# Sparse attention feeding a gated MLP: where batch 2's last products, the last x and the output stores are placed

## The chip, the core and the metric

The kernel runs on one core of one Trainium2 chip, in one launch. The core has TensorE (matrix products into PSUM), VectorE, ScalarE and GpSimd (elementwise work; GpSimd can't reach PSUM) and SyncE, which here only issues DMAs. The traces call them PE (with its weight loads as PEld), DVE, ACT, POOL and SP; SPq and ACTq are the DMA instructions that SyncE and ScalarE issue. The metric is the time of one execution on the device in microseconds (us), the median of several runs. Beside it stands one execution recorded by the hardware profiler, and its trace.

## The reference

For four batches, eight heads, 768 positions and a head size of 64, block-sparse attention is computed, and its result goes into a gated MLP with a spatial product (gMLP).

```python
scores = scale * np.matmul(q, k.transpose(0, 1, 3, 2))
mask = np.abs(blk_i - blk_j) <= window        # and first/last blocks, and 3 sampled blocks a row
scores = np.where(mask, scores, -1e9)
attn = softmax(scores)                        # exp, over the sum
x = (attn @ v).transpose(0, 2, 1, 3).reshape(B, S, H * D)

h = np.maximum(x @ w_in, 0.0)                 # 512 -> 1024
u, v = h[..., :512], h[..., 512:]
v_n = (v - v.mean(-1)) / np.sqrt(v.var(-1) + 1e-06)
v_s = np.einsum('ts,bsd->btd', w_spatial, v_n) + b_spatial[None, :, None]
out = (u * v_s) @ w_out
```

Inputs and output are float32; the kernel multiplies in bf16.

## The kernel before

**Attention.** The program is written as one list of slots (the loop at L880), and each engine works its instructions off in the order in which this loop issues them. Heads are taken in pairs; there are 16 pairs, four a batch, so pair 15 (heads 30 and 31 of 32) is the last of all. Slots 0 to 35 are a special start with thirds of the first batch. From slot 36 (`S0`) to 179 each slot does one chunk of 128 keys of one head: `qk_full` (L481) makes two matmuls of 384 columns into a scores' tile (PSUM tag "sc", two tiles) and ScalarE's exponential (L491). Seven slots later (`LAG`) `av_full` (L533) makes one AV group, six matmuls of 65 columns for one chunk of queries. After the sixth, `normalize` (L500) on VectorE divides by the sums (L502, L503) into xn. The last AV group of all, of head 31, is in slot 186.

**x.** gMLP wants x with features on the partitions, so a pair's xn is transposed into xt. For pairs up to 14, `xtr_dma` (L568) does this with a DMA transpose on SP's queue. For pair 15 `last_x` (L825) does it with six transposes on TensorE (L302) and two copies on VectorE.

**gMLP.** A batch is a list of steps, one matmul with 512 columns each (`product`, L608, the matmul at L615). For chunk t of six: v_t and u_t are four steps each (one for each pair of the batch, in the order of the pairs), s_t is six (the spatial product over all v), o_t is four. Together 108 steps. What follows a product:

- v_t: relu (in the last batch by ScalarE, L645), then on VectorE statistics and their aggregation (L650, L651). After each third v GpSimd computes 1/std of three chunks (L654, L656); from then on VectorE scales them, one at a time (L673, through the helper at L188), at step counts that are set when the third v closes (`vn_due`, `VN_AGE` 9, `VN_STEP` 2). What has not come up by s0 is scaled right before it.
- u_t: relu by ScalarE (L681).
- s_t: VectorE adds the bias and multiplies by u (L687). After s1, s3 and s5 a DMA transpose on SP's queue (L697) turns two chunks into `gt`, the input of the o products; in the last batch chunks 4 and 5 go one by one.
- o_t: a copy by ScalarE or VectorE into an output tile (`osb`), for batch 2 by ScalarE for t = 0, 2, 4; then a store (L716).

**Where the steps go.** `deal` (L742) queues a batch's steps and spreads them evenly over a number of slots; `run_queue` takes the next ones after the AV group of each slot. Batches 1 and 2 begin at slots 98 and 146, with 48 slots each. Within a slot the order is: scores, AV group, what `when` has put at this slot, then steps. In slot 188 `last_x` runs the rest of the queue at once (the leftovers of batch 2) and opens the last batch with the first three steps of v0, v1 and u0, before the fourth ones, which need pair 15's x. The rest of the last batch follows after the loop.

**PSUM.** `moe_ps` (L598) gives the tile for a product: within the slots in turn one of two gMLP tiles (names "ps_moe"). From `last_x` on (`ended`) it goes round three kinds: a scores' tile ("ps_sc"), an AV tile or a gMLP tile (both "ps_t").

**Weights.** w_spatial comes in six pieces, loaded by `ws_load` (L576) in slots 16 to 18: four single ones and the last two in one DMA. GpSimd casts them (L585) in slots 19 to 29.

Of the kernel before, what the change touches and what calls it, by code (L numbers as in the profile page):

```python
# [10 lines left out]
FP32 = mybir.dt.float32  # L11
# [15 lines left out]
def kernel(  # L27
# [16 lines left out]
    nc = tc.nc  # L44

    B, H, S, D = q.shape
# [3 lines left out]
    NCH = S // 128  # L50
# [6 lines left out]
    NG = H // 2  # L57
    NP = B * NG
# [6 lines left out]
    TW = TC * 128  # L65
    S0 = NT * NG * 3
# [4 lines left out]
    work = ctx.enter_context(tc.tile_pool(name="work", bufs=1))  # L71
    psum = ctx.enter_context(tc.tile_pool(name="psum", bufs=1, space=bass.MemoryType.PSUM))
# [147 lines left out]
    def dve_copy(o, i):  # L220
        nc.vector.tensor_copy(out=o, in_=i)  # L221
# [68 lines left out]
    moe_tags, held = deque(["moeA", "moeB"]), set()  # L290

    def moe_tag():
        moe_tags.rotate(1)
        if moe_tags[0] in held:
            moe_tags.rotate(1)
        return moe_tags[0]

    def bank(nm="ps", tag=None):
        return psum.tile([128, 1024], BF16, tag=tag or moe_tag(), bufs=2 if tag else 1, name=nm)

    def tr(ps, c, in_):
        nc.tensor.transpose(out=ps[:, c * 128:(c + 1) * 128], in_=in_, identity=ident)  # L302

    def pair_of(src, c):
        return src[:, c].rearrange("p h d -> p (h d)")
# [145 lines left out]
    a_ref, av_ref, x_ref, xn_ref, xt_ref = {}, {}, {}, {}, {}  # L451
# [96 lines left out]
    def xt_tile(p):  # L548
        if p not in xt_ref:
            xt_ref[p] = work.tile([128, S], BF16, tag="xt", bufs=7, name="xt")  # L550
        return xt_ref[p]
# [22 lines left out]
    ws = {}  # L574

    def ws_load(i, n=1):  # L576
        t = work.tile([128, n, S], FP32, tag=f"ws_f{n}", bufs=4 if n == 1 else 1, name="ws_f")
        nc.sync.dma_start(out=t, in_=moe_w_spatial.rearrange("(p c) s -> p c s", c=NCH)[:, i:i + n])
        for k in range(n):
            ws["f", i + k] = t[:, k]  # L580
# [17 lines left out]
    def moe_ps(last):  # L598
        if not (last or ended):
            return psum.tile([128, 512], FP32, tag=moe_tag(), bufs=1, name="ps_moe")  # L600
        tail_tags.rotate(1)
        if tail_tags[0] == "sc":
            return psum.tile([128, 1024], FP32, tag="sc", bufs=2, name="ps_sc")[:, 0:512]
        if tail_tags[0] == "moe":
            return psum.tile([128, 512], FP32, tag=moe_tag(), bufs=1, name="ps_t")
        return psum.tile([128, 512], FP32, tag="av", bufs=2, name="ps_t")

    def product(n, lhs, rhs, last, done, w=512):  # L608
        ref = {}
        out = []  # L610
        for i in range(n):
            def run(i=i):
                if i == 0:
                    ref["ps"] = moe_ps(last)
                nc.tensor.matmul(out=ref["ps"][:, 0:w], lhsT=lhs(i), rhs=rhs(i),  # L615
                                 start=(i == 0), stop=(i == n - 1))
                if i == n - 1:
                    done(ref["ps"][:, 0:w])
            out.append(run)
        return out  # L620
# [6 lines left out]
    class Moe:  # L627
# [75 lines left out]
        def o_product(self, tcc):  # L703
            steps = []
            osb = {}
            parts = 2 if self.last and tcc == NCH - 1 else 1
            w = DM // parts
            for i in range(parts):
                cs = slice(i * w, (i + 1) * w)

                def done(ps, i=i, cs=cs):
                    if i == 0:
                        osb["t"] = work.tile([128, DM], FP32, tag="osb", bufs=6, name="osb")
                    on_act = (tcc + i) % 2 == 0 if self.last else tcc in O_ACT[self.b]
                    (act_copy if on_act else dve_copy)(osb["t"][:, cs], ps)
                    (nc.scalar if i or (self.last and tcc == 0) else nc.sync).dma_start(  # L716
                        out=out[self.b].rearrange("(p c) d -> c p d", c=NCH)[tcc][:, cs],
                        in_=osb["t"][:, cs])
                steps += product(NDH, lambda d: self.gt[:, tcc, d, :],
                                 lambda d, cs=cs: w_out_t[:, d, cs], self.last, done, w)  # L720
            return steps
# [20 lines left out]
    def deal(steps, slots):  # L742
        queue.extend(steps)
        pace["slots"], pace["credit"] = slots, 0.0
# [14 lines left out]
    moe = {}  # L759
# [4 lines left out]
    def when(slot, *fns):  # L764
        at.setdefault(slot, []).extend(fns)

    def c(f, *a, **kw):
        return lambda: f(*a, **kw)
# [21 lines left out]
    def moe_begin(b):  # L790
        moe[b] = Moe(b)

    SEQ = "v0 v1 u0 v2 u1 v3 u2 v4 v5 u3 u4 u5"
# [21 lines left out]
    when(42, lambda: deal(moe[0].in_steps("v4 v5 u4 u5", TC) + moe[0].rest_steps(),  # L815
                          S0 + 8 + 48 - 42))
    for b in (1, 2):
        s0 = S0 + 48 * b + 14
        when(s0, c(moe_begin, b),
             lambda b=b: deal(moe[b].in_steps(SEQ, 3) + moe[b].rest_steps(), 48))  # L820

    last_steps = []


    def last_x():  # L825
        moe_begin(B - 1)
        m = moe[B - 1]
        ended.append(True)
        while queue:
            queue.popleft()()  # L830
        seq = m.in_steps("v0 v1 u0 v2 v3 v4 v5 u1 u2 u3 u4 u5", 3)
        n = NG - 1
        for i in (0, 1):
            for f in seq[i * NG:i * NG + n]:
                f()
        ps, xn = bank(), xn_ref.pop(("p", NP - 1))
        moe_tags.rotate(1)
        for cc in range(NCH):
            tr(ps, cc, pair_of(xn, cc))
        xt = xt_tile(NP - 1)  # L840
        for cs in (slice(0, TW), slice(TW, S)):
            dve_copy(xt[:, cs], ps[:, cs])
        for f in seq[2 * NG:2 * NG + n]:
            f()
        for i in (0, 1, 2):
            seq[i * NG + n]()
        last_steps.extend(seq[3 * NG:])

    def slot_of(p):
        return S0 + 12 * (p - NG)  # L850

    for p in range(NG, NP):
        g = slot_of(p)
        when({4: 13, 5: 22, 6: 31}.get(p, g - 34), c(load, p, "k"), c(load, p, "q"), c(load, p, "v"))
        when({4: 18, 5: 26, 6: 38}.get(p, g - 24),
             c(cast, p, "k", PL), c(cast, p, "q", PL), c(cast, p, "v", PL))
        when({4: 20, 5: 31}.get(p, g - (16 if p in (10, 14) else 20)), c(tr_dma, p))
        when(31 if p == 4 else g - (7 if p in (9, 13) else 5), c(split, p, 0))
        when(32 if p == 4 else g - 3, c(split, p, 1))
        if p == NP - 1:  # L860
            when(g + 20, last_x)
        else:
            when(g + (19 if p % NG == NG - 1 else 20), c(xtr_dma, p))
    for i, (ld, ca) in enumerate([(16, 19), (16, 21), (17, 23), (17, 25), (18, 27), (18, 29)]):
        if i < 5:
            when(ld, c(ws_load, i, 2 if i == 4 else 1))
        when(ca, c(ws_cast, i))
    for i, sl in enumerate((23, 27, 31)):
        when(sl, c(ws_tr, i))
# [60 lines left out]
```

## Time and profile before

| what | us |
|---|---|
| median of 3 runs | 209.9 (209.7 to 210.19) |
| the profiled execution | 209.46 |
| its span, first to last instruction | 207.7 |
| TensorE busy | 201.7 |
| ScalarE busy | 166.9 |
| VectorE busy | 128.9 |
| GpSimd busy | 74.5 |

Busy times are those of the span. Matmuls overlap in TensorE, so a row's length is more than its share: a matmul's time there is better read from the start of the next. A row of a timeline has the start, the length, the engine, the line, the operation, what it writes and reads, the count that was merged into it, and in brackets how long its engine had idled and what ended that. "Landing" is the time from a DMA's issue until its data has arrived.

### The profile page before, as it was taken

The page shows a single profiled execution, that of the slowest core. Times are in us where ns is not written, and L with a number is a line of the kernel's source. Part 1 is how long each engine was busy: PE and PEld are TensorE (multiplying, and loading weights), DVE is VectorE, ACT ScalarE, POOL GpSimd, SP SyncE. Part 2 cuts the span into 40 slices and gives each one's busy share as a digit, 9 for nine tenths or more (in the row PEclk, how much of TensorE's full clock was granted, in tenths as well). Part 3 has the DMA queues.
Part 4 walks back from the last instruction along what each step waited for, and adds up shares of the span by engine and source line. Part 5 has one row for each costly group of instructions (what it writes and reads, how often), then busy time and mean ns, then how long its engine had stood idle before and what let it go on. Part 6 is the DMA issues. An engine that isn't in the chain of part 4 may idle for free.

```text
span 207.7 us, 5257 instructions
## 1 busy us (share of the span) xinstructions
PE 201.7 (97%) x2128; PEld 126.8 (61%) x2128; DVE 128.9 (62%) x287; ACT 166.9 (80%) x222; POOL 74.5 (36%) x117
## 2 busy tenths in 40 slices
PE   7899999999999999999999999999999999999992
PEld 6689778756666666665556555556555655444441
DVE  7688697789644454558797445448785345476541
ACT  5999999999999999889999878988999882276021
POOL 6999898585680421400726303100201000012000
PEclk9999999999999999999999999999999999999999
DMA  5999999999999999999948548994101063810475
GB/s 138 355 364 365 359 402 248 234 270 332 275 292 246 206 302 209 324 282 280 298 54 225 143 91 261 189 267 91 31 3 38 3 88 67 286 55 0 50 186 219
DMA packets 65579, 42.21 MB, mean 203 GB/s; under 512 B 46740, under 2 KB 60436, under 8 KB 65556
## 3 DMA queue, kind: packets, MB, share of 16 engines
q1 hardware_dynamic: 64980, 41.30, 77.3%
q10 hardware_dynamic: 576, 0.59, 0.9%
q8 instruction: 16, 0.26, 0.5%
q14 instruction: 7, 0.06, 0.1%
HBM read 24.38 MB, written 6.29 MB: 148 GB/s over the span
## 4 chain that ended last, share of the span: by engine, by line
PE 92%; ACT 5%; DVE 1%; issue 0%; ACTq 0%
PE ps_moe L615 32%; PE ps L487 23%; PE ps_av L538 13%; PE ps_t L615 9%; PE ps L474 6%; ACT a_all L479 4%; PE ps_sc L615 4%; PE ps_av L520 4%; PE wps L182 1%; PE ps L302 1%; PE ps_av L302 1%; DVE osb L221 0%; ACT kq L224 0%; PE mq L309 0%; ACT osb L224 0%
## 5 line engine op out<-in xcount | busy, mean ns | idle before, releaser
L491 ACT ACTIVATE a_all<-ps 128x768 bf16<-128x768 f32 x144 | 112.7, 811 | 11.9 <-PE ps L487 5.4
L487 PE MATMUL ps<-kq 88*128 88x384 bf16 x288 | 70.4, 325 | 0.0
L538 PEld LDWEIGHTS <-a_all 128*128 128x128 bf16 x864 | 45.2, 97 | 20.0
L538 PE MATMUL ps_av<-vv,a_all 128*128 128x65 bf16 x864 | 49.8, 193 | 0.0
L487 PEld LDWEIGHTS <-kq 88*128 88x128 bf16 x288 | 27.8, 97 | 29.2 <-issue 0.3
L615 PE MATMUL ps_moe<-w_in_t,xt 128*128 128x512 bf16 x144 | 43.2, 378 | 0.0
L479 ACT ACTIVATE a_all<-ps 128x1024 bf16<-128x1024 f32 x36 | 34.1, 1028 | 1.8 <-PE ps L474 1.5
L615 PE MATMUL ps_moe<-vn,w_spt 128*128 128x512 bf16 x108 | 33.5, 378 | 0.0
L654 POOL TENSOR_SCALAR std<-mv 128x3 f32<-128x3 f32 (+1 forms) x9 | 2.9, 318 | 71.7 <-DVE mv L651 57.1
L138 POOL CAST nat<-st_k 128x768 bf16<-128x768 f32 (+2 forms) x18 | 13.8, 770 | 31.3 <-DMA st_k<-in_k_dram 31.0
L502 DVE RECIPROCAL rc<-ps_av 128x6 f32<-128x6 f32 (+1 forms) x36 | 6.7, 187 | 26.5 <-PE ps_av L538 23.7
L687 DVE SCALAR_TENSOR_TENSOR un<-ps_moe,b_col,un 128x512 bf16<-128x512 f32 x18 | 13.5, 749 | 14.8 <-PE ps_moe L615 14.8
L474 PE MATMUL ps<-kq 88*128 88x256 bf16 (+3 forms) x140 | 21.6, 275 | 1.0 <-ACT a_all L479 0.5
L615 PEld LDWEIGHTS <-xt 128*128 128x128 bf16 x192 | 15.4, 98 | 7.5 <-DVE xt L221 0.2
L503 DVE TENSOR_TENSOR xn<-ps_av,rc 128x384 bf16<-128x384 f32 (+1 forms) x36 | 18.5, 513 | 1.2
L615 PE MATMUL ps_moe<-w_out_t,gt 128*128 128x512 bf16 x60 | 17.6, 378 | 0.0
L650 DVE BATCH_NORM_STATS2 stats<-vn 128x6 f32<-128x512 bf16 x24 | 16.4, 684 | 1.3 <-ACT vn L645 0.9
L474 PEld LDWEIGHTS <-kq 88*128 88x128 bf16 (+1 forms) x140 | 12.7, 97 | 5.4 <-DVE kq L221 1.0
L138 POOL CAST nat<-st_q 128x768 bf16<-128x768 f32 (+2 forms) x21 | 14.4, 688 | 2.7 <-DMA st_q<-in_q_dram 2.2
L188 DVE TENSOR_SCALAR vn<-ps_moe 128x512 bf16<-128x512 f32 x18 | 12.3, 686 | 4.6 <-PE ps_moe L615 4.5
L615 PEld LDWEIGHTS <-w_spt 128*128 128x128 bf16 x144 | 11.7, 98 | 5.2
L221 DVE COPY kq<-tt 64x1536 bf16<-64x1536 bf16 x24 | 13.9, 581 | 0.4
(85 smaller groups left out, 207.4 us busy)
## 6 DMA issues: line engine op xcount, KB each, us to landing
st_v<-in_v_dram SPq DMA_DIRECT2D x16, 384.0 KB, 5.6
st_k<-in_k_dram SPq DMA_DIRECT2D x15, 384.0 KB, 4.7
out_dram<-osb SPq DMA_DIRECT2D x22, 256.0 KB, 2.7
st_q<-in_q_dram SPq DMA_DIRECT2D x12, 384.0 KB, 4.6
w_f<-in_moe_w_in_dram SPq DMA_DIRECT2D x6, 256.0 KB, 6.7
ws_f<-in_moe_w_spatial_dram SPq DMA_DIRECT2D x4, 384.0 KB, 7.3
w_f<-in_moe_w_out_dram SPq DMA_DIRECT2D x4, 256.0 KB, 4.0
st_q<-in_q_dram SPq DMA_DIRECT2D x6, 128.0 KB, 5.3
```

The costliest lines, as they stand in the source:

```text
L138: eng.tensor_copy(out=dst, in_=src)
L188: nc.vector.tensor_scalar(out=out, in0=in0, scalar1=s1, scalar2=s2, op0=o0, **kw)
L221: nc.vector.tensor_copy(out=o, in_=i)
L474: nc.tensor.matmul(out=ps[:, at:at + n * TW], lhsT=kq[0:kr, h, ci * 128:(ci + 1) * 128], rhs=kq[0:kr, h, qcols(t0, n)], start=True, stop=True)
L479: nc.scalar.activation(out=out, in_=ps, func=AF.Exp, scale=0.125)
L487: nc.tensor.matmul(out=ps[:, hf * 512:hf * 512 + HALF], lhsT=kq[0:KR, j % H, ci * 128:(ci + 1) * 128], rhs=kq[0:KR, j % H, S + hf * HALF:S ...
L491: nc.scalar.activation(out=a_ref["h", j][:, ci, :].rearrange("p (b c) -> p b c", b=2), in_=ps.rearrange("p (b c) -> p b c", b=2)[:, :, 0:H ...
L503: nc.vector.tensor_tensor(out=out, in0=ps[:, :, 0:D], in1=rc[:, 0:n].to_broadcast([128, n, D]), op=ALU.mult)
L538: nc.tensor.matmul(out=av_ref[j][:, qc, 0:VA], lhsT=a_ref["h", j][:, ci, qc * 128:(qc + 1) * 128], rhs=vv[p % NVV][:, h, ci, 0:VA], start= ...
L615: nc.tensor.matmul(out=ref["ps"][:, 0:w], lhsT=lhs(i), rhs=rhs(i), start=(i == 0), stop=(i == n - 1))
L650: nc.vector.bn_stats(out=stats, in_=self.vn[:, tcc, :])
L687: nc.vector.scalar_tensor_tensor(out=self.un[:, tcc, :], in0=ps, scalar=b_col[:, tcc:tcc + 1], in1=self.un[:, tcc, :], op0=ALU.add, op1=AL ...
```

## The change

Six edits.

1. `moe_ps`: batch 2's leftovers in slot 188 take scores' tiles alone (two of them, in turn); the last batch goes round the three kinds as before.
2. Pair 15's x is made by `xtr_dma`, in slot 186, right behind the AV group there; TensorE's six transposes and the two copies go. Pairs 7 and 11 move from 19 to 18 slots after their first one.
3. The last batch begins v0 v1 v2 u0 instead of v0 v1 u0 v2; the three products opened ahead are v0, v1, v2.
4. Batch 2's gMLP begins at slot 150 instead of 146, still over 48 slots; batch 1's is spread over 52.
5. The stores of o1 and o2 of the last batch are issued by ScalarE, as that of o0 was.
6. Pieces 2 and 3 of w_spatial come in one DMA, as 4 and 5 did.

```diff
     def ws_load(i, n=1):
-        t = work.tile([128, n, S], FP32, tag=f"ws_f{n}", bufs=4 if n == 1 else 1, name="ws_f")
+        t = work.tile([128, n, S], FP32, tag=f"ws_f{n}", bufs=2, name="ws_f")
...
     def moe_ps(last):
         if not (last or ended):
             return psum.tile([128, 512], FP32, tag=moe_tag(), bufs=1, name="ps_moe")
+        if not last:
+            return psum.tile([128, 1024], FP32, tag="sc", bufs=2, name="ps_sc")[:, 0:512]
         tail_tags.rotate(1)
...
-                    (nc.scalar if i or (self.last and tcc == 0) else nc.sync).dma_start(
+                    (nc.scalar if i or (self.last and tcc < 3) else nc.sync).dma_start(
...
     for b in (1, 2):
-        s0 = S0 + 48 * b + 14
+        s0 = S0 + 48 * b + (14 if b == 1 else 18)
         when(s0, c(moe_begin, b),
-             lambda b=b: deal(moe[b].in_steps(SEQ, 3) + moe[b].rest_steps(), 48))
+             lambda b=b: deal(moe[b].in_steps(SEQ, 3) + moe[b].rest_steps(), 52 if b == 1 else 48))
...
-        seq = m.in_steps("v0 v1 u0 v2 v3 v4 v5 u1 u2 u3 u4 u5", 3)
-        n = NG - 1
-        for i in (0, 1):
+        seq = m.in_steps("v0 v1 v2 u0 v3 v4 v5 u1 u2 u3 u4 u5", 3)
+        n, opened = NG - 1, 3
+        for i in range(opened):
             for f in seq[i * NG:i * NG + n]:
                 f()
-        ps, xn = bank(), xn_ref.pop(("p", NP - 1))
-        moe_tags.rotate(1)
-        for cc in range(NCH):
-            tr(ps, cc, pair_of(xn, cc))
-        xt = xt_tile(NP - 1)
-        for cs in (slice(0, TW), slice(TW, S)):
-            dve_copy(xt[:, cs], ps[:, cs])
-        for f in seq[2 * NG:2 * NG + n]:
-            f()
-        for i in (0, 1, 2):
+        for i in range(opened):
             seq[i * NG + n]()
-        last_steps.extend(seq[3 * NG:])
+        last_steps.extend(seq[opened * NG:])
...
+        when(g + (18 if p % NG == NG - 1 else 20), c(xtr_dma, p))
         if p == NP - 1:
             when(g + 20, last_x)
-        else:
-            when(g + (19 if p % NG == NG - 1 else 20), c(xtr_dma, p))
     for i, (ld, ca) in enumerate([(16, 19), (16, 21), (17, 23), (17, 25), (18, 27), (18, 29)]):
-        if i < 5:
-            when(ld, c(ws_load, i, 2 if i == 4 else 1))
+        if i not in (3, 5):
+            when(ld, c(ws_load, i, 2 if i > 1 else 1))
```

## The prediction

> **What bounds the kernel now.** I read the page first, then the chain of waits near its end, then the timelines of single engines after the last scores, at 170 us and later.
>
> ```profile
> PE 201.7 (97%) x2128; PEld 126.8 (61%) x2128; DVE 128.9 (62%) x287; ACT 166.9 (80%) x222; POOL 74.5 (36%) x117
> PE 92%; ACT 5%; DVE 1%; issue 0%; ACTq 0%
> ```
>
> TensorE is busy for 97% of the span and is 92% of the chain that ended last. The ends of matmuls are modelled, so I check it by starts. In the chain, by start and length:
>
> ```profile
> 176.62 0.69 DVE osb L221
> ...
> 181.40 0.34 PE ps L302 x6
> ...
> 190.80 2.59 PE ps_t L615 x12
> ```
>
> A gMLP step (one matmul with 512 columns) takes 2.59/12 = 0.216 us. The six transposes of pair 15's x take 0.34 us. Once, at 176.62, the chain leaves TensorE for a copy of an output tile (o1) by VectorE, which holds a PSUM bank. What this costs stands in TensorE's own timeline:
>
> ```profile
> 173.87 0.59 PE L615 MATMUL ps_moe<-w_out_t,gt 128*128 128x512 bf16 x2
> 174.30 0.35 PE L538 MATMUL ps_av<-vv,a_all 128*128 128x65 bf16 x6
> 174.49 0.59 PE L615 MATMUL ps_moe<-w_out_t,gt 128*128 128x512 bf16 x2
> 174.92 0.34 PE L538 MATMUL ps_av<-vv,a_all 128*128 128x65 bf16 x6
> 175.10 0.60 PE L615 MATMUL ps_moe<-w_out_t,gt 128*128 128x512 bf16 x2
> 175.54 0.34 PE L538 MATMUL ps_av<-vv,a_all 128*128 128x65 bf16 x6
> 175.72 1.46 PE L615 MATMUL ps_moe<-w_out_t,gt 128*128 128x512 bf16 x6
> 177.36 0.81 PE L615 MATMUL ps_t<-w_out_t,gt 128*128 128x512 bf16 x3 [0.18 <-DVE osb L221]
> ```
>
> Six steps from 175.72 end at 175.72 + 6 x 0.216 = 177.02, and the next starts at 177.36: a hole of 0.34 us. Elsewhere in these rows starts follow each other by steps alone. So TensorE is the limit, and the change can only take away matmuls or holes, or make new holes. Moving steps from one slot to another is neutral as long as nothing else becomes the limit.
>
> **The change, part by part.**
>
> *x of pair 15 by DMA* takes six transposes from TensorE: -0.34 us. Its landing (2.7 to 2.8 us for such transposes late in the run, row below) is covered by 16 steps of leftovers, 3.45 us, and nine of the last batch; without that cover what is missing of the 2.8 us would stand before v0's fourth step.
>
> *Leftovers in the scores' tiles.* The hole of 0.34 us was a wait for the bank of o1; o2 and o3 now get scores' tiles, which no exponential uses any more: -0.34 us. But there are two such tiles for five products, so o3 waits for o1's copy. By the o1 copy below (0.68 us on VectorE) it ends about 3.46 us, and o3 wants to start at 3.43 us, after the last AV group's start; with 0.06 us from copy to matmul (177.30 to 177.36) that is +0.09. Bounds: nothing, and 0.34 again.
>
> *Batch 2 four slots later.* By the kernel's own dealing arithmetic 22 steps instead of 13 are left when slot 188 flushes the queue. The slots between get fewer steps: batch 1 has 108 steps in 52 slots, 2.08 a slot.
>
> ```profile
> 110.53 1.52 ACT L491 ACTIVATE a_all<-ps 128x768 bf16<-128x768 f32 x2
> 111.93 0.60 ACT L681 ACTIVATE un<-ps_moe 128x512 bf16<-128x512 f32 x1
> ```
>
> Two exponentials back to back take 111.93 - 110.53 = 1.40 us, so ScalarE needs 0.70 us a slot and at most 0.60 more for a copy. TensorE needs 2.08 x 0.216 + 0.18 (AV, 175.54 to 175.72) + two score matmuls of 0.16 (384/512 of a step) = 0.95 us. ScalarE stays below it: no cost, and up to 0.3 us if three u copies in a row were uncovered.
>
> The cost lies at the end. s5 of batch 2 now ends in slot 187, right behind the last AV group of slot 186, and o4 and o5 read what the DMA transpose of chunks 4 and 5 writes after s5. On SP's queue this transpose now stands *behind* the new transpose of pair 15, which waits for head 31's normalisation.
>
> ```profile
> 174.14 0.75 DVE L687 SCALAR_TENSOR_TENSOR un<-ps_moe,b_col,un 128x512 bf16<-128x512 f32 x1 [0.68 <-PE ps_moe L615]
> ...
> 176.15 0.56 DVE L503 TENSOR_TENSOR xn<-ps_av,rc 128x384 bf16<-128x384 f32 x1
> 176.62 0.68 DVE L221 COPY osb<-ps_moe 128x512 f32<-128x512 f32 x1
> ```
> ```profile
> 174.92 1.23 SPq L697 DMA_TRANSPOSE gt<-un  x1
> ```
> ```profile
> 198.19 2.54 SPq L697 DMA_TRANSPOSE gt<-un  x2
> ```
> ```profile
> gt<-un SPq DMA_TRANSPOSE x1, 3.3
> ```
> ```profile
> DMA to landing us min/median/max: 2.5/3.4/4.2
> ```
> ```profile
> DMA to landing us min/median/max: 2.7/2.8/2.8
> ```
>
> The third of these is the landing of the pair issued between 196 and 198 us; the fourth that of all 13 gt transposes, the last that of the x transposes after 100 us. Count from the end of s5, which is the last AV group's start plus 0.18 plus three steps, 0.83 us. *DMA path*: head 31's xn ends 1.17 us after that AV group's start (175.54 to 176.71), so at 0.34. SP issues 0.03 later (174.89 to 174.92), at 0.37, and is held for 1.23: 1.60. The next issue follows after 0.08 (2.54 - 2 x 1.23), at 1.68; s5's own multiplication (0.75, behind xn) is done by then, at 1.09. Landing 3.3 later: 4.98. I take 3.3 of 2.5 to 4.2 because there, too, another transpose was in flight. *TensorE's path*: 16 steps, 3.45, plus 0.09: 3.54. **Hole before o4: +1.44** (0.64 to 2.34 by the landing's ends). In the kernel before, s5 ended at 173.87, three AV groups and the hole lay in between, and SP was free at once: there a landing of 3.3 would have just met o4, at 174.92 + 3.3 against 177.36 + 4 x 0.216 = 178.22. That cover is what the change uses up. Behind the waiting weights load stands all of the last batch; on SP, behind the pair, the stores of batch 2, for which nobody waits.
>
> A rule speaks for a shorter landing. A window of half a microsecond inside the data of such a pair, with the rate in GB/s last:
>
> ```profile
> 172.00:172.50 0.50, 0.50 (x9) 0.35 (x8) 0.45 (x2) 0.00 (x0) 0.00 (x0) 1.00 1.11 214
> ```
>
> At 214 GB/s the pair's 262 KB take 1.22 us. The Trainium skill ("DMA: Bandwidth & Descriptors", Latency and other measured facts) gives DMA transposes with contiguous rows about 350 to 400 GB/s. By that page I estimate 0.7 us for the data and a hole smaller by 0.5; the trace disagrees with its 214, and decides.
>
> *v2 ahead of u0 in the last batch.* Its normalisations run on VectorE in the order of the program. Write S for a chunk's statistics, V for its scaling. Before: S0 S1 S2 S3 S4 V0 V1 S5 V2. v2 now closes at step 12 instead of 16, its scalings are due at steps 20, 22 and 24, so: S0 S1 S2 S3 V0 V1 S4 V2 S5.
>
> ```profile
> 185.58 0.18 DVE L651 BATCH_NORM_AGGREGATE mv<-stats 128x2 f32<-128x6 f32 x1
> ...
> 186.38 0.18 DVE L651 BATCH_NORM_AGGREGATE mv<-stats 128x2 f32<-128x6 f32 x1
> ...
> 187.27 0.70 DVE L188 TENSOR_SCALAR vn<-vn,mv,rstd 128x512 bf16<-128x512 bf16 x2
> ...
> 190.18 1.06 DVE L188 TENSOR_SCALAR vn<-vn,mv,rstd 128x512 bf16<-128x512 bf16 x3 [1.09 <-POOL rstd L656]
> ```
> ```profile
> 186.17 0.88 POOL L656 TENSOR_TENSOR rstd<-std,mhalf 128x3 f32<-128x3 f32 x1
> ```
> ```profile
> 190.64 1.67 PE L615 MATMUL ps_t<-vn,w_spt 128*128 128x512 bf16 x7
> ```
>
> VectorE runs this stretch without a break. Now V0 stands after S3 and needs GpSimd's result, 187.05 - 185.58 = 1.47 us after S2's aggregation starts; S3 takes only 0.80 of it (185.58 to 186.38) and about 0.1 to the next start, so VectorE waits about 0.6. One scaling more (0.70/2 = 0.35) stands ahead of S5. The last V ends 0.6 + 0.35 later against TensorE. It ended at 191.24, and the sixth step of s0, which reads it, started at 190.64 + 5 x 0.216 = 191.72: a margin of 0.48. **Hole in s0: +0.5.** Bounds: 0 (all within the margin) and 0.7.
>
> *Stores 1 and 2 by ScalarE.* Each costs its queue 0.35 us:
>
> ```profile
> 200.15 0.35 ACTq L716 DMA_DIRECT2D out_dram<-osb  x1
> 201.25 0.60 ACT L224 ACTIVATE osb<-ps_sc 128x512 f32<-128x512 f32 x1 [1.13 <-PE ps_sc L615]
> ```
>
> Store 1 waits there for VectorE's copy, and ScalarE's copy of o2 waits behind it, about 0.2 us; ScalarE idles 1.13 us ahead of that copy, and o2's bank is not needed again. Cover gone, it would cost 0.35 once. I take 0. *The merged weight piece* and pair 7's and 11's x one slot earlier:
>
> ```profile
> 36.10 0.90 POOL L138 CAST nat<-st_k 128x768 bf16<-128x768 f32 x1 [0.74 <-DMA st_k<-in_k_dram]
> ```
>
> GpSimd's cast of the third piece may wait for the fourth, now in the same transfer; GpSimd idles 0.74 us at 36 us and swallows that. SP waits up to one slot longer on the two x transposes, with about eight slots until o4 of the batch ahead reads its own. I take 0, bounds -0.2 and +0.3.
>
> **The sum:** -0.34 - 0.34 + 0.09 + 1.44 + 0.5 = +1.35 us. The profiled execution took 209.46 us (span 207.7); it becomes 210.8. The three timed runs have a median of 209.9, 0.44 above it, so I predict 209.9 + 1.4 = **211.3 us**; with landings of 3.0 to 3.8 and the ends of the small terms, 210.8 to 212.0.
>
> **Rivals.** (a) *Only the hole before o4*: VectorE's chain keeps its margin, the 0.5 goes: 210.8. For: a 0.48 margin exists. Against: the new order is fixed by step counts. (b) *A short landing*: with the lowest, 2.5 us, the hole is 0.64 and the sum +0.55: 210.5. For: the row has it. Against: single chunks, half the data, are among the 13. The rate on the page of the Trainium skill named above ("DMA: Bandwidth & Descriptors") points this way, and the window's 214 GB/s against it. (c) *The pair lands in time*, the other side: if chunks 4 and 5 land under 1.86 us after their issue (3.54 - 1.68), there is no hole at o4. Then -0.59 remains, 209.3; with VectorE's 0.5 it is 209.8. It decides from a hole of 0.59 downward. For: the kernel before shows no wait at o4. Against: no landing below 2.5. (d) *A slow issue*: one gt transpose held SP for longer,
>
> ```profile
> 165.43 2.45 SPq L697 DMA_TRANSPOSE gt<-un  x1
> ```
>
> and 1.2 us more before o4 gives 212.5.
>
> **Chances.** Forecast 0.58, (a) 0.10, (b) 0.08, (c) 0.18, split 0.12 at 209.3 and 0.06 at 209.8, (d) 0.06. About 0.2%, 0.42 us, is what a measurement of this kernel can tell from no change. So faster 0.12, same 0.06, slower 0.82. Leaving out (c)'s faster part and (d), 0.18 together, the range is 209.8 to 212.0.
>
> **What would show it.** The six transposes and the 0.34 hole gone; about 0.1 before o3 on a scores' tile; a weights load of o4 waiting on the gt DMA for about 1.4 us, with the pair's issue right behind pair 15's; V0 waiting for GpSimd after S3, and s0's fourth to sixth steps late by 0.5 in all. Wrong it would be if o4 starts on time, if V0 does not wait, or if holes appear between 100 and 170 us, where I expect none.

## The result, and the profile after

The changed kernel takes **210.68 us** (10 runs, 210.32 to 210.94) beside 209.93 of the kernel before (10 runs, 209.59 to 210.31). The ratio of the times is 1.0034, with a 95% interval of 1.0025 to 1.0044: slower by 0.75 us, where +1.4 was forecast. The time lies inside the range of 209.8 to 212.0, and just under the narrower one of 210.8 to 212.0 that went with the forecast itself.

The page of the changed kernel: the span, the busy times, and the shares of the chain that ended last.

```profile
span 208.9 us, 5244 instructions
...
PE 202.2 (97%) x2122; PEld 126.5 (61%) x2122; DVE 129.6 (62%) x285; ACT 166.7 (80%) x222; POOL 73.9 (35%) x117
...
PE 87%; DVE 4%; ACT 4%; DMA 1%; POOL 1%; issue 1%; POOLq 0%; ACTq 0%
```

TensorE has six instructions fewer, the transposes. Its share of the chain fell from 92% to 87%; a DMA and GpSimd have come in, and VectorE's share has grown. The chain itself, by start and length, shows where:

```profile
176.58 3.10 DMA gt<-un
179.73 1.90 PE ps_sc L617 x8
...
187.36 0.89 POOL rstd L658
188.28 0.73 DVE vn L188 x2
```

The first line is the transpose that o4 waits for, the second o4 and o5 behind it; the last two are GpSimd's result and V0, which waits for it. How much of them is idle TensorE stands in its timeline (start, length, and in brackets the idle time and what ended it):

```profile
174.05 0.34 PE L538 MATMUL ps_av<-vv,a_all 128*128 128x65 bf16 x6
...
174.87 1.03 PE L617 MATMUL ps_moe<-w_out_t,gt 128*128 128x512 bf16 x4
175.74 2.83 PE L617 MATMUL ps_sc<-w_out_t,gt 128*128 128x512 bf16 x12
179.73 1.90 PE L617 MATMUL ps_sc<-w_out_t,gt 128*128 128x512 bf16 x8 [1.16 <-DMA gt<-un]
```

A row of n steps without a gap has the length 0.216 n + 0.16; the 0.16 is the modelled drain of the last one. Twelve would take 2.75, and the second row has 2.83: a hole of 0.08 lies in it, the one before o3. Its last step gives way at 175.74 + 2.83 - 0.16 = 178.41, and the next starts at 179.73: a hole of 1.32 before o4. SP's queue shows why:

```profile
175.28 1.21 SPq L569 DMA_TRANSPOSE xt<-xn  x1
176.58 1.26 SPq L699 DMA_TRANSPOSE gt<-un  x1
```

The gt transpose of chunks 4 and 5 is issued 0.09 us after pair 15's has let SP go, and lands 3.10 later. And s0 and s1 of the last batch, in TensorE's timeline once more:

```profile
191.83 3.23 PE L617 MATMUL ps_t<-vn,w_spt 128*128 128x512 bf16 x12
194.89 1.46 PE L617 MATMUL ps_sc<-vn,w_spt 128*128 128x512 bf16 x6
```

Twelve steps in 3.23 instead of 2.75: 0.48 us of holes (three of 0.26, 0.11 and 0.11). VectorE's timeline has their origin:

```profile
186.78 0.18 DVE L653 BATCH_NORM_AGGREGATE mv<-stats 128x2 f32<-128x6 f32 x1
186.87 0.66 DVE L652 BATCH_NORM_STATS2 stats<-vn 128x6 f32<-128x512 bf16 x1
187.57 0.18 DVE L653 BATCH_NORM_AGGREGATE mv<-stats 128x2 f32<-128x6 f32 x1
188.28 0.73 DVE L188 TENSOR_SCALAR vn<-vn,mv,rstd 128x512 bf16<-128x512 bf16 x2 [0.53 <-POOL rstd L658]
```

V0 waits 0.53 us for GpSimd behind S3 (186.87 to 187.75) and starts 1.50 us after the aggregation of S2 has started.

On TensorE the change therefore costs -0.34 - 0.34 + 0.08 + 1.32 + 0.48 = +1.20 us. The time grew by 0.75 only. The other 0.45 is not on TensorE; the experiments had to find it.

### The profile page after: what moved, and what is told of

Same layout as the page of the kernel before. It is cut to its first block, busy times and chain, and to the rows that moved or that the text cites. A ratio compares the mean times of both kernels' runs of the same rounds, so it can differ in the third digit from the quotient of the medians.

```text
span 208.9 us, 5244 instructions
## 1 busy us (share of the span) xinstructions
PE 202.2 (97%) x2122; PEld 126.5 (61%) x2122; DVE 129.6 (62%) x285; ACT 166.7 (80%) x222; POOL 73.9 (35%) x117
## 4 chain that ended last, share of the span: by engine, by line
PE 87%; DVE 4%; ACT 4%; DMA 1%; POOL 1%; issue 1%; POOLq 0%; ACTq 0%
PE ps_moe L617 31%; PE ps L487 23%; PE ps_av L538 13%; PE ps L474 6%; PE ps_t L617 5%; PE ps_av L520 4%; PE ps_sc L617 3%; ACT a_all L479 3%; DVE stats L652 1%; DMA gt<-un 1%; PE wps L182 1%; DVE kq L221 1%; DVE vn L188 1%; PE ps_av L302 1%; DVE mv L653 0%
## 5 line engine op out<-in xcount | busy, mean ns | idle before, releaser
L656 POOL TENSOR_SCALAR std<-mv 128x3 f32<-128x3 f32 (+1 forms) x9 | 2.4, 270 | 72.5 <-DVE mv L653 70.3
L617 PE MATMUL ps_moe<-w_out_t,gt 128*128 128x512 bf16 x52 | 15.6, 378 | 0.0
L221 DVE COPY kq<-tt 64x1536 bf16<-64x1536 bf16 x24 | 14.4, 598 | 0.3
```

## The experiments

Each kernel was timed beside the kernel before; a ratio stands with its 95% interval. The sum over a profile is made with the last row of TensorE and the span; the time of the profiled executions is 1.8 to 2.0 us above their spans.

### The kernel before, once more

The kernel is unchanged.

> The kernel before, unchanged, for a second profile of it. Theory: the holes that TensorE has after 20 us are fixed by the order of the program (0.34 us before o3 of batch 2, none in s0 of the last batch), and the profile shown of before is 0.47 us under its median because of its first ten microseconds, where it has 3.34 us of holes and the changed kernel 3.79. So the holes after 170 us stay within 0.1 us of 0.40 + 0.14, the first ten microseconds may move by half a microsecond, and the last 0.36 us stall of SyncE after all landings comes again or not, which tells whether it belongs to the kernel. Rival: o4 of batch 2 is a near miss in the kernel before (landing 0.3 us ahead of need), so in other executions it too waits at o4; then a hole of 0.1 to 0.5 us stands there. Time: ratio 1.000, 209.9 us.

Measured: 209.99 us, ratio 0.9995 (0.9981 to 1.0010). This profile, at 209.99, has the median's time, where the one on which the prediction rests was 0.5 under it. The six steps and o3, as predicted from the other one at 175.72 and 177.36:

```profile
176.22 1.46 PE L615 MATMUL ps_moe<-w_out_t,gt 128*128 128x512 bf16 x6
177.86 1.89 PE L615 MATMUL ps_t<-w_out_t,gt 128*128 128x512 bf16 x8 [0.18 <-DVE osb L221]
```

The hole is the same (177.86 - 176.22 - 1.30 = 0.34), and both rows stand 0.50 later: the difference arose in the first 6 us of the trace, and has nothing to do with the part that is changed. Adding the sum to the median, not to the profiled time, was the right choice.

### The order of the last batch put back

```diff
-        seq = m.in_steps("v0 v1 v2 u0 v3 v4 v5 u1 u2 u3 u4 u5", 3)
+        seq = m.in_steps("v0 v1 u0 v2 v3 v4 v5 u1 u2 u3 u4 u5", 3)
```

> The changed kernel with the last batch's order v0 v1 u0 v2 put back (opened ahead: v0, v1, u0). Theory: the three holes in s0 (0.26 + 0.11 + 0.11 us) come from V0 waiting behind S3 for GpSimd and one scaling more ahead of S5; they go, nothing else changes: 0.48 us less than the changed kernel, 210.2 us. The hole before o4 stays at 1.2 to 1.4 us. Rival: what is late in s0 only moves on, to the gt transposes before o2 and o5 of the last batch; then the time stays at 210.7.

Measured: 210.08 us, ratio 1.0002 (0.9990 to 1.0015); 0.60 less than the changed kernel. TensorE's timeline of this kernel:

```profile
191.94 2.75 PE L617 MATMUL ps_t<-vn,w_spt 128*128 128x512 bf16 x12
194.53 1.46 PE L617 MATMUL ps_sc<-vn,w_spt 128*128 128x512 bf16 x6
```

Twelve steps in 2.75, no hole; the one before o4 stays at 1.32. So the +0.5 in s0 is caused by the order alone.

### Pair 15's transpose issued behind that of chunks 4 and 5

```diff
+        if p == NP - 1:
+            late.setdefault(g + 19, []).append(c(xtr_dma, p))
+        else:
+            when(g + (18 if p % NG == NG - 1 else 20), c(xtr_dma, p))
-        when(g + (18 if p % NG == NG - 1 else 20), c(xtr_dma, p))
```

> The changed kernel with the DMA transpose of pair 15's x issued behind that of chunks 4 and 5 of batch 2 (end of slot 187 in place of slot 186). Theory: the transpose of chunks 4 and 5 then starts when s5's multiplication ends, 1.12 us after the end of s5 instead of 1.71, lands 3.15 later, and the hole before o4 shrinks from 1.32 to about 0.7 us: 210.1 us. Pair 15's x lands about 5.2 us after s5 and is needed at 7.9. Rival: the landing and not the queue sets it, or two transposes in flight slow each other in this order too; then the hole stays over 1.1 us and the time at 210.6 or more.

Measured: 210.17 us, ratio 1.0019 (1.0002 to 1.0037). SP and TensorE:

```profile
176.57 1.23 SPq L699 DMA_TRANSPOSE gt<-un  x1
177.90 1.26 SPq L569 DMA_TRANSPOSE xt<-xn  x1
```
```profile
176.81 2.40 PE L617 MATMUL ps_sc<-w_out_t,gt 128*128 128x512 bf16 x10
179.83 1.90 PE L617 MATMUL ps_sc<-w_out_t,gt 128*128 128x512 bf16 x8 [0.62 <-DMA gt<-un]
```

The hole is now 179.83 - (176.81 + 2.40 - 0.16) = 0.78. It fell by 0.54, and the median time by 0.51. The times alone would not carry this: the interval overlaps that of the changed kernel (1.0025 to 1.0044), and the profiled execution, at 210.74, is not shorter, since its TensorE had fallen 0.5 us behind already between 31 and 39 us, far ahead of the edit. The hole is the evidence. So 0.54 of the 1.32 is the place behind pair 15's issue, and 0.78 is there without it: then s5's own multiplication, behind xn on VectorE, sets the issue (it ends at 176.54).

### Batch 2 back at its old slots, the rest of the change kept

```diff
-        s0 = S0 + 48 * b + (14 if b == 1 else 18)
+        s0 = S0 + 48 * b + 14
...
-             lambda b=b: deal(moe[b].in_steps(SEQ, 3) + moe[b].rest_steps(), 52 if b == 1 else 48))
+             lambda b=b: deal(moe[b].in_steps(SEQ, 3) + moe[b].rest_steps(), 48))
```

> The changed kernel with batch 2 at its old place (slot 146, batches 1 and 2 over 48 slots each); all other edits stay. Theory: s5 ends in slot 183 with three AV groups behind it and SyncE free, so the hole before o4 falls to 0 to 0.35 us; the hole before o3 (0.34 before) stays gone, the six transposes stay gone, the 0.48 us in s0 stay. So 1.0 to 1.3 us under the changed kernel: 209.4 to 209.7 us, at or just under the kernel before. Rival: the shift was needed to cover pair 15's x, and without it the wait moves to the fourth step of v0; then a hole of a microsecond stands there and the time is 210.5.

Measured: 210.04 us, ratio 0.9997 (0.9985 to 1.0008): a miss, although the hole before o4 is down to 0.13 as expected. New ones stand before o2 and o5 of the last batch:

```profile
199.06 1.89 PE L617 MATMUL ps_t<-w_out_t,gt 128*128 128x512 bf16 x8
201.17 1.04 PE L617 MATMUL ps_sc<-w_out_t,gt 128*128 128x512 bf16 x4 [0.22 <-DMA gt<-un]
202.04 1.89 PE L617 MATMUL ps_t<-w_out_t,gt 128*128 128x512 bf16 x8
204.07 0.61 PE L617 MATMUL ps_sc<-w_out_t,gt 128*128 128x256 bf16 x4
```

Eight steps from 199.06 end at 200.79, four from 201.17 at 202.03, eight from 202.04 at 203.77: holes of 0.38 and 0.30. They wait for gt, and gt for s3's multiplication, which VectorE does late. Its rows of s2 and s3, with the idle time ahead of each in brackets:

```profile
195.44 0.75 DVE L689 SCALAR_TENSOR_TENSOR un<-ps_sc,b_col,un 128x512 bf16<-128x512 f32 x1 [0.55 <-PE ps_sc L617]
197.09 0.75 DVE L689 SCALAR_TENSOR_TENSOR un<-ps_t,b_col,un 128x512 bf16<-128x512 f32 x1 [0.90 <-PE ps_t L617]
```

A spatial product comes every 1.30 us (6 x 0.216), and s3's multiplication starts 1.65 after s2's: 0.35 late. In the kernel before it is s2's that is late by this, and nobody waits for s2 alone:

```profile
195.15 0.75 DVE L687 SCALAR_TENSOR_TENSOR un<-ps_sc,b_col,un 128x512 bf16<-128x512 f32 x1 [0.90 <-PE ps_sc L615]
```

Counting all of VectorE's records of a trace from zero, semaphore waits included, the late one is number 319, in this kernel as in that; here two records fewer stand ahead, so it falls on s3.

### Two records more on VectorE

The kernel of the last experiment, with two writes to a tile that nobody reads, in slot 100:

```diff
+    pad = const.tile([128, 1], FP32, name="pad")
...
+    for _ in range(2):
+        when(100, c(nc.vector.memset, pad, 0.0))
```

> The changed kernel with batch 2's place put back, as the earlier run with that alone, and nothing else but the two tiny memsets on VectorE in slot 100. Theory (lateness sits at a row of VectorE's stream, whatever stands there): the 0.35 us fall on s2's multiplication, which nobody waits for, the holes before o2 and o5 fall from 0.39 and 0.30 to 0.04 and 0.08, the three in s0 stay at 0.48: 0.5 us less than that run, 209.5 us. Rival (the lateness belongs to s3, or to a DMA that s3 waits for): no change, 210.0 us.

Measured: 209.72 us, ratio 0.9990 (0.9979 to 1.0002), 0.32 under the one without them; the two intervals overlap, so the reading rests on the trace. VectorE's s2, which now has the long wait of 0.90, and TensorE's rows to set beside those above:

```profile
195.76 0.75 DVE L690 SCALAR_TENSOR_TENSOR un<-ps_sc,b_col,un 128x512 bf16<-128x512 f32 x1 [0.90 <-PE ps_sc L618]
```
```profile
199.02 1.89 PE L618 MATMUL ps_t<-w_out_t,gt 128*128 128x512 bf16 x8
200.75 1.03 PE L618 MATMUL ps_sc<-w_out_t,gt 128*128 128x512 bf16 x4
```

More work on VectorE, and less time: the late one is s2's again, and the hole before o2 is gone (200.75 - 199.02 = 8 x 0.216). That before o5 fell from 0.30 to 0.11. The last matmul starts 0.62 earlier than without the two writes, of which the time shows half; the span after that matmul is 0.2 longer, because the last store, issued by ScalarE, takes 2.0 us to its landing in place of 1.8. Why it does was not tested.

### The stores alone

The kernel before with edit 5 only:

```diff
-                    (nc.scalar if i or (self.last and tcc == 0) else nc.sync).dma_start(
+                    (nc.scalar if i or (self.last and tcc < 3) else nc.sync).dma_start(
```

> The kernel before with edit 5 alone: the stores of o1 and o2 of the last batch issued by ScalarE. In both profiles of the kernel before SyncE stalls for 0.36 us in its last steps, after all data has landed; in those of the changed kernel it takes 0.06. SyncE's trace has 211 rows in the kernel before and 207 in the changed one. Theory: the stall belongs to a place in SyncE's instruction stream (about its 207th row), and a kernel whose stream ends ahead of it is spared it and 0.1 us that follow; taking two stores away is enough. So TensorE's end stays where it was, and the time falls by 0.3 to 0.45 us: 209.5 to 209.6. Rival: the 0.4 us come with something else of the change (the merged load, x of pair 15); then 209.9, as before.

Measured: **209.49 us**, ratio 0.9982 (0.9970 to 0.9995). This is the term that the prediction put at nothing. The last row of TensorE and the span, first of the kernel before (its second profile), then of the stores alone, then of the changed kernel:

```profile
span 208.2 us, 5257 instructions
...
203.80 0.60 PE L615 MATMUL ps_t<-w_out_t,gt 128*128 128x256 bf16 x4
```
```profile
span 207.9 us, 5255 instructions
...
203.98 0.60 PE L615 MATMUL ps_t<-w_out_t,gt 128*128 128x256 bf16 x4
```
```profile
204.94 0.60 PE L617 MATMUL ps_t<-w_out_t,gt 128*128 128x256 bf16 x4
```

From the end of TensorE's last matmul to the end of the span: 208.2 - 204.4 = 3.8, then 207.9 - 204.6 = 3.3, then 208.9 - 205.5 = 3.4 us. The difference lies among SyncE's closing instructions. Its drains (shortest, median and longest in ns; start of the first and last), in the same order of kernels:

```profile
L925 SPq DRAIN  x3: 7/7/130, 207.0 to 207.7; - x3
```
```profile
L925 SPq DRAIN  x3: 7/7/7, 207.2 to 207.5; - x3
```
```profile
L917 SPq DRAIN  x3: 7/7/7, 208.2 to 208.5; - x3
```

In the kernel before the three take from 207.0 to 207.7, one of them 130 ns; in the other two 0.3 us and 7 ns each. SyncE issues no store in that stretch, and the last one has landed by about 207.0: it stalls for some 0.4 us on its own. It has 211 records in the kernel before, 207 in the other two.

### Four records more on SyncE

The changed kernel with four small DMAs in slot 100, to a tile that nobody reads:

```diff
+    for i in range(4):
+        when(100, c(nc.sync.dma_start, out=pad[:, i:i + 1], in_=b_col[:, i:i + 1]))
```

> The changed kernel with four more DMAs on SyncE's queue in slot 100, 512 bytes each from one tile on the core to another that nobody reads. SyncE's stream gets its length of before back (211 rows instead of 207, or some more for waits); nothing on TensorE, VectorE or ScalarE changes, and the queue has time to spare there. Theory: the place in the stream where SyncE stalls falls into the program's end again, after the last data has landed; the time from TensorE's last matmul to the end goes from 3.4 back to 3.8 us: 211.1 us. Rival: the 0.4 us belong to which engine issues the last stores; then 210.7.

Measured: 211.51 us, ratio 1.0081 (1.0067 to 1.0095); 0.83 more than the changed kernel. SyncE has 211 records again, TensorE ends where it did, and the drains of this kernel are like those of the kernel before:

```profile
span 209.7 us, 5247 instructions
...
204.91 0.60 PE L618 MATMUL ps_t<-w_out_t,gt 128*128 128x256 bf16 x4
```
```profile
L921 SPq DRAIN  x3: 7/13/111, 208.5 to 209.2; - x3
```

So the stall comes back with the count of SyncE's records. The run-out is now 209.7 - 205.5 = 4.2 us, twice the growth that I expected. The rest lies in SyncE's closing waits for the stores (time in all, how many, the longest), here of the changed kernel and then of this one:

```profile
SPq L917 <- DMA out_dram<-osb: 1.7, 2, 1.5
```
```profile
SPq L921 <- DMA out_dram<-osb: 2.0, 1, 2.0
```

Ahead of its drains SyncE has five closing waits. In the changed kernel the fifth is the one for the last store, which lands at 208.08. Here it is the first: each DMA raises one of eight semaphores in turn, and four DMAs more have shifted which one the last store raises. So four waits that ran ahead of the landing now run behind it (it is at 208.09), which takes the other 0.3 us. The edit thus changed two things at the end, and the drains tell them apart. It also left VectorE with one record fewer; number 319 is a semaphore wait there, and none of the multiplications is late.

### Order and slots put back, with the tiles, x by DMA and the stores kept

```diff
-        s0 = S0 + 48 * b + (14 if b == 1 else 18)
+        s0 = S0 + 48 * b + 14
...
-        seq = m.in_steps("v0 v1 v2 u0 v3 v4 v5 u1 u2 u3 u4 u5", 3)
+        seq = m.in_steps("v0 v1 u0 v2 v3 v4 v5 u1 u2 u3 u4 u5", 3)
```

> The changed kernel with both put back, the order v0 v1 u0 v2 and batch 2's place. Theory: no holes in s0; o4 waits 0.13 us as in the run with the place alone put back; 0.68 us of transposes and bank wait stay saved. But that run had two new holes, 0.39 before o2 and 0.30 before o5 of the last batch, since VectorE's multiplication for s3 started 0.35 us late: in all six profiles VectorE is late by 0.35 us at row 319 of its trace, which is s2's multiplication where two more instructions stand ahead of it and s3's here. These come again. Sum against the kernel before: -0.68 + 0.13 + 0.04 (before o3) + 0.35 + 0.22 = +0.05, less up to 0.4 at the run-out: 209.6 to 209.9 us. Rival: what was late there came from s0's holes; then 209.2.

Measured: 209.51 us, ratio 0.9976 (0.9966 to 0.9987), just under the expected range. Holes of 0.13 before o4, and of 0.40 and 0.33 before o2 and o5 of the last batch: VectorE's late record is s3's here too.

### The tiles alone, and pair 15's x alone

The kernel before with edit 1 only:

```diff
+        if not last:
+            return psum.tile([128, 1024], FP32, tag="sc", bufs=2, name="ps_sc")[:, 0:512]
```

> The kernel before with edit 1 alone: batch 2's leftovers in scores' tiles. Theory: the hole of 0.34 us before o3 goes, o4 comes 0.34 us earlier and meets its transpose 0.1 to 0.15 us before it lands: 0.2 us less than before, 209.7 us; VectorE's and SyncE's streams keep their lengths, so nothing moves elsewhere. Rival: the bank was not what o3 waited for; then the hole stays and the time is 209.9.

Measured: 209.80 us, ratio 0.9994 (0.9985 to 1.0002), within what can be told from no change. TensorE's timeline of this kernel:

```profile
176.44 1.46 PE L617 MATMUL ps_moe<-w_out_t,gt 128*128 128x512 bf16 x6
177.73 2.89 PE L617 MATMUL ps_sc<-w_out_t,gt 128*128 128x512 bf16 x12
```

The hole of 0.34 is gone (177.73 - 176.44 = 6 x 0.216). Of this 2.89 - 2.75 = 0.14 comes back within the twelve steps, before o4, which now comes early enough to meet the landing of gt. What the trace gains is some 0.2 us.

The kernel before with pair 15's x by DMA in slot 186 and v0, v1, u0 opened:

```diff
-        for i in (0, 1):
+        for i in (0, 1, 2):
...
-        for cc in range(NCH):
-            tr(ps, cc, pair_of(xn, cc))
...
+            when(g + 18, c(xtr_dma, p))
```

> The kernel before with pair 15's x by DMA alone (issued in slot 186; opened ahead v0, v1, u0; order, tiles, place and stores as before). Theory: TensorE loses six transposes, 0.34 us, and the hole of 0.34 before o3 stays. But VectorE loses two copies, so row 319 of its stream becomes s3's multiplication and the holes before o2 and o5 of the last batch grow by 0.35 and 0.25; SyncE's stream has two rows more and its stall at the end stays. -0.34 + 0.60: 210.2 us, slower than before although both engines do less. Rival (rows have nothing to do with it): 0.34 less, 209.6 us.

Measured: 210.01 us, ratio 1.0005 (0.9992 to 1.0018): six transposes less on TensorE, and no gain. Its o2 and o5 of the last batch:

```profile
200.49 1.04 PE L615 MATMUL ps_sc<-w_out_t,gt 128*128 128x512 bf16 x4 [0.22 <-DMA gt<-un]
...
203.49 0.61 PE L615 MATMUL ps_sc<-w_out_t,gt 128*128 128x256 bf16 x4 [0.24 <-DMA gt<-un]
```

With the drain of 0.16 these are holes of 0.38 and 0.40. Two copies fewer on VectorE (the edit removes them) put its late record on s3: on TensorE the gain of 0.34 is more than given back, at a place that the edit doesn't touch.

### The best of both

Order and slots put back, two records added on VectorE, and two stores of batch 2 moved from SyncE to ScalarE (206 records on SyncE):

```diff
-                    (nc.scalar if i or (self.last and tcc < 3) else nc.sync).dma_start(
+                    (nc.scalar if i or (self.last and tcc < 3) or (self.b == 2 and tcc in (3, 5))
+                     else nc.sync).dma_start(
```

> As the run with order and place put back, and two tiny VectorE memsets of a tile that nobody reads in slot 100 (VectorE is free there), so that row 319 is s2's multiplication again; and the stores of o3 and o5 of batch 2 by ScalarE, so that SyncE's stream is two rows shorter. Theory: the holes before o2 and o5 go back to 0.04 and 0.08, the stall at the run-out goes: -0.68 + 0.13 + 0.04 - 0.43 = -0.9 us against the kernel before, 209.0 us. Rival (the rows have nothing to do with it): the two holes stay and the time is that of the run without these two edits.

Measured: **208.92 us**, ratio 0.9952 (0.9940 to 0.9964): faster than the kernel before and the changed one, and 0.59 under the run without these two edits, so the rival is out. Its TensorE around o4:

```profile
177.88 2.90 PE L618 MATMUL ps_sc<-w_out_t,gt 128*128 128x512 bf16 x12
180.62 1.46 PE L618 MATMUL ps_t<-w_in_t,xt 128*128 128x512 bf16 x6
```

Twelve steps in 2.90: of the holes before o3, before o4 and in s0, only some 0.15 before o4 is left; the hole before o2 is gone, too, and 0.11 stands before o5. The last attempt takes the one before o4 away, with batch 2 two slots *earlier* than before:

```diff
-        s0 = S0 + 48 * b + 14
+        s0 = S0 + 48 * b + (14 if b == 1 else 12)
...
-             lambda b=b: deal(moe[b].in_steps(SEQ, 3) + moe[b].rest_steps(), 48))
+             lambda b=b: deal(moe[b].in_steps(SEQ, 3) + moe[b].rest_steps(), 46 if b == 1 else 48))
```

> As the best run so far, with batch 2 two slots earlier than in the kernel before (slot 144, batch 1 over 46 slots). Theory: s5 then ends in slot 181 with five AV groups between it and o4, two steps of 0.19 us more than before, so the last hole before o4 (0.13 us) goes; pair 15's x lands 3.95 us after the last AV group's start and is needed at 4.9. 0.13 us less: 208.8 us. Rival: the wait moves to the fourth step of v0, or ScalarE or VectorE becomes late in the slots that now carry 2.35 steps; then 209.0 or more.

Measured: 209.20 us, ratio 0.9966 (0.9954 to 0.9978). The trace has no hole before o4:

```profile
178.62 1.89 PE L618 MATMUL ps_sc<-w_out_t,gt 128*128 128x512 bf16 x8
180.35 1.46 PE L618 MATMUL ps_t<-w_in_t,xt 128*128 128x512 bf16 x6
```

Yet the median time isn't lower, though the profiled span is (207.2 for 207.5). The intervals of the two overlap (five runs each), so which of them is faster is not settled.

## Why the prediction was right, and where it was off

The direction, the mechanism and each hole on TensorE came as predicted; the time was 0.6 us too high, because one term was put at nothing that was worth -0.4, and two were 0.12 and 0.02 too large. By its own steps:

- *x of pair 15 by DMA*, -0.34: right on TensorE, and its landing was covered. What the prediction did not see is that the edit alone, with two instructions fewer on VectorE, moves a stall to where it hurts (210.01 alone). With batch 2 in its new slots, as in the changed kernel, it is s2's again.
- *Leftovers in the scores' tiles*, -0.34 and +0.09: the hole went, and 0.08 came before o3.
- *Batch 2 four slots later*, **+1.44**: 1.32. From the end of s5 (the start of the AV group at 174.05 plus 0.83: 174.88) pair 15's issue comes 0.40 later (predicted 0.37), that of chunks 4 and 5 at 1.70 (1.68); TensorE's path is 3.53 (3.54). The landing is 3.1 for 3.3, which alone would leave 1.27; the other 0.05 pass from the landing (176.58 + 3.10) to o4's first matmul at 179.73, a step that the sum did not have. The experiment with the two issues exchanged divides the hole: 0.54 by the queue, 0.78 by the moved s5. With batch 2 back in its slots 0.13 is left.
- The rule in the Trainium skill ("DMA: Bandwidth & Descriptors", Latency and other measured facts), 350 to 400 GB/s for such transposes, would make this hole smaller by an estimated 0.5, so 0.94. The trace has 1.32, a landing of 3.1, and inside the data of that transpose, from 178.30 to 178.80 us, a rate of 211 GB/s: it does not bear the rule out here.
- *v2 ahead of u0*, +0.5: 0.48, and 0.60 by the times when the order alone is put back. V0 waits 0.53 (0.6).
- *Stores 1 and 2 by ScalarE*: "**I take 0**". This step failed. It is worth -0.4: alone it gives 209.49 beside 209.88, and with it SyncE's closing stall is gone, which comes back with four records more and the same stores. The prediction looked at what the stores cost their new queue, and not at what their absence does to the old one. It had no view of the time after TensorE's last matmul at all, 3.8 us of the span.
- *The merged weight piece* and pairs 7 and 11, taken as 0: no new hole shows in TensorE's trace between 100 and 170 us, and from 13 to 90 us it keeps one distance (0.45 us) to that of the kernel before. By themselves they were not tried.

The sum on TensorE is +1.20 for +1.35 predicted, and -0.4 at the end makes +0.8 of it, beside +0.75 measured. The rivals: (a) needed s0 without a hole, (b) a landing of 2.5, (c) one under 1.86, (d) an SP held for 2.45 at an issue; none of the four is what the traces show. That (a) and (b) give 210.8 and 210.5, nearer to 210.68 than the forecast, is chance: their mechanism did not happen.

## What to carry to other kernels

When work is moved behind the last cover, count each instruction that its consumer needs, through every queue: here a DMA transpose behind another one cost 0.54, and the move itself some 0.65 (0.78 less the 0.13 that is there without it); the hole could be read beforehand to 0.12 us. Read the run-out too, from the last matmul to the end of the span, with the engine that closes it. And before an edit is judged by its time alone, see whether a stall elsewhere has only changed its place: pair 15's x alone took 0.34 us of work from TensorE and gained nothing, and with batch 2 put back TensorE ended 0.62 earlier once two useless writes on VectorE had moved the stall away.

## What the runs showed of the hardware

**Stalls that stand at a place of an engine's instructions.** Count an engine's records in a trace from zero, semaphore waits included. VectorE's number 319 starts 0.35 us late in thirteen of the fourteen profiles: it is the multiplication of s2 in nine of them, of s3 in the three that have two records fewer ahead of it, of s1 where batch 2 comes two slots earlier. In the fourteenth, with four more DMAs on SyncE, it is a semaphore wait in which VectorE idles anyway, and no multiplication is late. SyncE's number 207 starts 0.3 us late in the eight profiles that have one there among further closing waits and drains, and where it is a drain it takes 0.1 longer as well. Kernels with 208 records or fewer are spared, those with 211 or more are not; with 209 about 0.2 is left of it at the end.

The page of the changed kernel has a queue that may belong to this:

```profile
q14 instruction: 7, 0.06, 0.1%
```

Its seven packets of 8 KB are instructions. The last of the seven starts 0.7 to 1.1 us after VectorE's late record has started, in all thirteen profiles, while that record stands anywhere between 193.9 and 197.1 us. One packet more starts 0.6 to 0.9 us after SyncE's late record; in the kernels that are spared it starts only 0.6 to 1.9 us after the span's end. (The packets' clock may be off by up to 0.4 us.) Both packets start after the late record, so neither is one that the engine was waiting for. An engine that comes to the end of a block of its instructions, and asks for a further block just then, would fit both. That adding two records to VectorE moves its stall, and four to SyncE brings its own back, was shown; the loading itself was not changed by any run, and this cause stays a guess.
